# Unread products on TensorE during the first batch entry's attention, and two score banks in place of three

## The chip, the cores and the metric

One NeuronCore of a Trainium2 chip runs the whole program. The metric is the device time in microseconds (us); each kernel has several runs and their median is given. A difference of about 0.2% is what these runs can tell from none. One further execution was recorded by the hardware profiler, and all rows below come from it.

## What is computed

Three parts run one after another on the same 1152 tokens (2 batch entries of 576). The first is an attention of 8 heads, which adds a coarse attention over tokens averaged by fours to a local one with a band mask:

```python
out_d = sm_attn(q_d, k_d, v_d)            # 144 averaged tokens
out_up = np.repeat(out_d, factor, axis=2)
mask = np.abs(pos[:, None] - pos[None, :]) < factor
scores = np.where(mask, scale * np.matmul(q, k.transpose(0, 1, 3, 2)), -1000000000.0)
...
return (out_up + out_local).astype(np.float32)
```

The second is a mixture of 8 experts (512 to 1024 to 512, ReLU, gates balanced by 8 rounds of row and column scaling), the third a dense layer pair (512 to 2048 to 512, softplus).

## The kernel before, in words

**Attention.** A `Unit` is a pair of heads of one batch entry; there are four per entry, eight in all. `load` issues its copies on SyncE (queries and keys into `qk`, values into `vw` and `vd`). `setup(g)`, called for g = 0, 1, 2, transposes three tiles of `qk` on TensorE (line 322) into a PSUM tile `tb`; VectorE sums it by fours (`qkd`, line 327), scales that into `flat` (line 333) and copies half of the queries into `fine` (line 338); ScalarE writes `kT` (line 337) and the other half of `fine` (line 339). `scores(blk)` works on one of four blocks: "c" is the coarse attention (line 355), 0 to 2 are the local one (a mask product in bf16, line 362, and products of `fine` with `kT`, line 368). VectorE takes the maxima (line 375), ScalarE the exponentials (line 379), VectorE sums, reciprocals and the scaling (lines 380 to 382). `turn` transposes the result (lines 393, 402) and ScalarE copies it out (lines 397, 403); `values` multiplies by the values (lines 413, 424) and VectorE adds both attentions (line 439). Blocks go through `scores`, `turn` two blocks later and `values` three blocks later.

**Banks.** `bank("m", ...)` hands out three PSUM banks, `m0`, `m1`, `m2`, in turn. In the first batch entry (`self.b == 0`) the scores of each block take the next of them; in the second entry they use another tag. From the second entry on, `m0` to `m2` serve the experts' first products (line 601, `product`, by the table `places`).

**Overlap.** The loop over `stream` runs the 32 blocks. From block 18 on (`begin`) it also draws from `beside()`, which does the first expert's work on TensorE between the attention of the second entry. In the first entry TensorE has only attention to do. Beside all this, `fetch_first` and `fetch_second` load weights (SyncE) and split them into a high and a low part: ScalarE copies, VectorE (line 133) and GpSimd (lines 111, 139, 154) subtract and add.

**Order.** Tile's scheduler decides the order of each engine's instructions when the program is built, by priorities that follow the order in the source and by a model of when operands are ready. An engine then works through its list strictly in that order. `tc.keep_in_program_order` puts an instruction behind the one that was written before it on the same engine; `tc.high_priority(offset=...)` shifts its priority, and a negative offset makes it less urgent than what stands around it. After the attention, TensorE's order is written out by hand (`manual_schedule`).

Of the kernel before, what the change touches and what calls it, by code (L numbers as in the profile page):

```python
# [9 lines left out]
F32 = mybir.dt.float32  # L10
F32R = mybir.dt.float32r
U32 = mybir.dt.uint32
BF16 = mybir.dt.bfloat16
# [7 lines left out]
def attention_moe_mlp(ctx: ExitStack, tc: tile.TileContext, q, k, v, w_gate, w1, w2, w_in, w_out, out):  # L21
    nc = tc.nc
    B, H, S, D = q.shape
    NT, DM = out.shape
    E, _, FF = w1.shape
    F2 = w_out.shape[0]
    P = 128
# [4 lines left out]
    NQ = S // QT  # L32
    NB = 3
    CT = SD // NB
    KW = QT + 2 * R
    KD = DM // P
    SCALE = 1.0 / float(D) ** 0.5
# [25 lines left out]
    ps = ctx.enter_context(tc.tile_pool(name="ps", bufs=1, space=PSUM))  # L63

    def bank(tag, name):
        if tag == "m":
            tag = f"m{next(turns) % 3}"
        return ps.tile([P, 512], F32, tag=tag, bufs=4 if tag == "at" else 1, name=name)

    turns = count()  # L70
# [182 lines left out]
    at = tc.tile_pool(name="at", bufs=2)  # L253
    ap = at.__enter__()


    identb = ap.tile([P, P], BF16, bufs=1, name="identb")
    nc.vector.tensor_copy(identb, ident)

    mask = ap.tile([P, NB + 2, KW], BF16, bufs=1, name="mask")  # L260
    nc.gpsimd.memset(mask, 0.0)
    for t0, t1, off in ((0, 1, 0), (1, NB + 1, R), (NB + 1, NB + 2, 2 * R)):

        for hh in range(2):
            part = mask[hh * QT : (hh + 1) * QT, t0:t1, :]
            for sign in (1, -1):
                nc.gpsimd.affine_select(
                    out=part, in_=part, compare_op=ALU.is_gt, fill=NEG,
                    base=R + sign * off, pattern=[[0, t1 - t0], [-sign, KW]], channel_multiplier=sign,
                )  # L270
    rest = const.tile([P, KD, LEFT], F32, name="rest")

    fine = [ap.tile([P, NB, 2, QT], F32, bufs=1, name=f"fine{g}") for g in range(NB)]
    flat = [ap.tile([P, NB, 2, CT], F32, bufs=1, name=f"flat{i}") for i in range(2)]
    for x in fine + flat:
        nc.gpsimd.memset(x, 0.0)

    class Unit:
# [9 lines left out]
        def bank(self, name, kind):  # L288
            return bank(("m", "at", "y")[kind] if self.b == 0 else "at", name)

        def load(self, first=False):
# [3 lines left out]
            for cut in cuts:  # L295
                for w, src in enumerate((q, k)):
                    for hh in range(2):
# [3 lines left out]
                        )  # L301
            self.vw = vw = ap.tile([KW, NQ, 2, D], F32, tag="vw", name="vw")
            for t, w0 in ((0, 0), (NQ - 1, S - KW)):
                nc.sync.dma_start(vw[:, t], v[b, h0 : h0 + 2, w0 : w0 + KW, :].rearrange("h p d -> p h d"))
            for hh in range(2):
                src = v[b, h0 + hh, QT - R :, :]
                windows = bass.AP(tensor=src.tensor, offset=src.offset, ap=[[D, KW], [QT * D, NQ - 2], [1, D]])
                nc.sync.dma_start(vw[:, 1 : NQ - 1, hh], windows)
# [40 lines left out]
        def scores(self, blk):  # L349

            sc = self.bank("sc", 0)
            if blk == "c":
                rows, w = 2 * CT, SD
                for i in range(NB):
# [30 lines left out]
        def turn(self, blk):  # L385

            ex = self.state[blk]
            if blk == "c":
                et = ap.tile([HC, 2, NB * 2 * CT], F32, tag="etc", bufs=1, name="etc")
                for c in range(2):  # L390
                    tp = self.bank("tp", 1)
                    for i in range(NB):
                        nc.tensor.transpose(
                            tp[:HC, i * 2 * CT : (i + 1) * 2 * CT], ex[:, i, c * HC : (c + 1) * HC],
                            ident[: 2 * CT, : 2 * CT],
                        )
                    nc.scalar.copy(et[:, c], tp[:HC, : NB * 2 * CT])
            else:
# [65 lines left out]
    def gates():  # L464
        lg = bank("y", "lg")
        for s in range(2):
            lts = pair("lts").rearrange("p a c -> p (a c)")[: 2 * E]
            for j in range(2):
                lt = bank("at", "lt")
                terms = [  # L470
                    (i, w, kk, x[s]) for i, w in (((4, 1), (5, 2)), ((3, 0), (1, 1)))[j]
                    for kk in range(2) for x in (xh, xl)
                ]
                for n, (i, w, kk, x) in enumerate(terms):
                    nc.tensor.matmul(
                        lt[: 2 * E, : HALF[s]], wgs[:, w, kk, :], x[:, i, kk, :],
                        start=(n == 0), stop=(n == len(terms) - 1),
                    )
                nc.scalar.copy(halves(s, lts)[j], lt[: 2 * E, : HALF[s]])
            for t in TILES[s]:  # L480
                o = t * P - T0[s]
                nc.tensor.matmul(lg[:, t * E : (t + 1) * E], lts[:, o : o + P], fold, start=True, stop=True)
        nc.vector.tensor_reduce(m1, lg[:, : NTT * E], axis=AX.X, op=ALU.max)
        nc.vector.tensor_copy(prf, lg[:, : NTT * E])
# [49 lines left out]
    for e, g, s, p in steps:  # L534
        m = e * NP + p
# [205 lines left out]
    for n in range(len(stream) + LAG + 1):  # L741
        if n < len(stream):
            x, blk = stream[n]
            i, j = divmod(n, len(blocks))
            x.scores(blk)
            if j == 1 and 1 <= i <= 6:
                (fetch_first if i % 2 else fetch_second)((i - 1) // 2, (i - 1) // 2)
            if j >= 2 and i + 1 < len(units):
                for g in ((0, 1), (2,))[j - 2]:
                    units[i + 1].setup(g)  # L750
                if j == 3 and i + 2 < len(units):
                    units[i + 2].load()
        for lag, what in ((LAG, "turn"), (LAG + 1, "values")):
            if 0 <= n - lag < len(stream):
                x, blk = stream[n - lag]
                getattr(x, what)(blk)
        while columns < (n - begin) * DENSE:
            columns += next(side, 1 << 30)
# [100 lines left out]
```

## Time and profile before

| | |
|---|---|
| median of 3 runs | 1095.72 us (1094.87 to 1096.78) |
| span of the profiled execution | 1094.7 us, 17873 instructions |
| TensorE matmul busy | 1060.0 us, 97% of the span |
| VectorE / ScalarE / GpSimd busy | 727.0 / 555.2 / 537.6 us |
| first product of an expert (line 601) starts | 66.70 us |

The profiled span lies 1.0 us below the median, and within 0.2 us of the fastest run. The page gives busy time by engine, and in 40 slices also the clock that TensorE was granted (tenths of full speed). In the rows, PE is TensorE's matmul queue, PEld its weight loads, DVE VectorE, ACT ScalarE, POOL GpSimd and SP SyncE; in a group of instructions the mean duration of one stands behind the busy time. An interval written in square brackets is idle time ahead of an instruction, with what ended it.

### The profile page before, as it was taken

The page shows a single profiled execution, that of the slowest core. Times are in us where ns is not written, and L with a number is a line of the kernel's source. Part 1 is how long each engine was busy: PE and PEld are TensorE (multiplying, and loading weights), DVE is VectorE, ACT ScalarE, POOL GpSimd, SP SyncE. Part 2 cuts the span into 40 slices and gives each one's busy share as a digit, 9 for nine tenths or more (in the row PEclk, how much of TensorE's full clock was granted, in tenths as well). Part 3 has the DMA queues.
Part 4 walks back from the last instruction along what each step waited for, and adds up shares of the span by engine and source line. Part 5 has one row for each costly group of instructions (what it writes and reads, how often), then busy time and mean ns, then how long its engine had stood idle before and what let it go on. Part 6 is the DMA issues. An engine that isn't in the chain of part 4 may idle for free.

```text
span 1094.7 us, 17873 instructions
## 1 busy us (share of the span) xinstructions
PE 1060.0 (97%) x6385; PEld 938.0 (86%) x6385; DVE 727.0 (66%) x1532; ACT 555.2 (51%) x1443; POOL 537.6 (49%) x569
## 2 busy tenths in 40 slices
PE   6899999999999999999999999999999998999998
PEld 5678888998987889888888988898898897889987
DVE  6889665565666676667657665766663578766765
ACT  4667645343444444434444443444443567676763
POOL 6735235464467676756766455354664212222321
PEclk9579999999999999999999999999999999999999
DMA  8454101111235334434443332223333273244112
GB/s 175 118 115 109 49 27 55 62 58 40 84 100 145 115 110 143 132 105 127 122 134 102 117 112 93 100 93 110 102 116 116 106 278 139 113 175 182 68 39 87
DMA packets 133497, 119.70 MB, mean 109 GB/s; under 512 B 35744, under 2 KB 111776, under 8 KB 133408
## 3 DMA queue, kind: packets, MB, share of 16 engines
q1 hardware_dynamic: 133408, 118.56, 35.0%
q8 instruction: 50, 0.82, 0.3%
q14 instruction: 39, 0.32, 0.1%
HBM read 93.11 MB, written 25.43 MB: 108 GB/s over the span
## 4 chain that ended last, share of the span: by engine, by line
PE 40%; POOL 5%; DMA 5%; DVE 3%; issue 2%; ACT 2%; SPq 0%; POOLq 0%; ACTq 0%; DVEq 0%
PE yps L660 21%; PE m L601 19%; DMA raw<-in_moe_w_out 2%; POOL sums L111 2%; POOL w2l L154 1%; POOL cva L188 1%; POOL cva L197 1%; DMA raw<-in_moe_w 1%; DMA raw<-in_moe_w_in 1%; DVE cva L178 1%; POOL w1l L139 1%; DVE cva L189 0%; DVE cva L179 0%; DVE cva L182 0%; DMA s_out<-cva 0%
## 5 line engine op out<-in xcount | busy, mean ns | idle before, releaser
L601 PE MATMUL m<-xh,w1h 128*128 128x320 f32 (+1 forms) x1120 | 336.6, 301 | 13.1 <-ACT t L610 6.3
L601 PE MATMUL m<-xh,w1l 128*128 128x320 f32 (+1 forms) x1120 | 332.5, 297 | 0.0
L601 PE MATMUL m<-xl,w1h 128*128 128x320 f32 (+1 forms) x1120 | 332.4, 297 | 0.0
L601 PEld LDWEIGHTS m<-xh,w1h 128*128 128x128 f32 x1120 | 212.2, 189 | 38.7 <-ACT t L610 10.8
L601 PEld LDWEIGHTS m<-xl,w1h 128*128 128x128 f32 x1120 | 212.4, 190 | 11.8
L601 PEld LDWEIGHTS m<-xh,w1l 128*128 128x128 f32 x1120 | 212.2, 190 | 0.2 <-issue 0.2
L660 PE MATMUL yps<-w2h,hh 128*128 128x512 f32 x502 | 198.5, 395 | 0.0
L660 PE MATMUL yps<-w2l,hh 128*128 128x512 f32 x502 | 198.4, 395 | 0.0
L660 PE MATMUL yps<-w2h,hl 128*128 128x512 f32 x502 | 195.5, 389 | 0.0
L660 PE MATMUL yps<-w2h,h 128*128 128x512 f32 x436 | 153.3, 393 | 0.0
L615 DVE TENSOR_TENSOR c<-m,t 128x256 f32<-128x256 f32 (+1 forms) x160 | 72.3, 452 | 100.9 <-PE m L601 99.5
L139 POOL TENSOR_TENSOR w1l<-sums,w1h 128x512 fp32r<-128x512 f32 x72 | 95.8, 1345 | 78.2 <-ACT w1h L138 54.4
L571 POOL TENSOR_TENSOR ab<-ab,up 128x320 f32<-128x320 f32 (+1 forms) x64 | 53.9, 843 | 157.2 <-ACT ln L567 109.8
L154 POOL TENSOR_TENSOR w2l<-raw,w2h 128x512 fp32r<-128x512 f32 x72 | 94.9, 1339 | 71.4 <-ACT w2h L153 71.3
L558 ACT ACTIVATE hh<-c 128x256 fp32r<-128x256 f32 (+1 forms) x138 | 60.0, 443 | 125.0 <-DVE c L615 123.3
L559 DVE SCALAR_TENSOR_TENSOR hl<-c,hh 128x256 fp32r<-128x256 f32 (+1 forms) x138 | 91.4, 668 | 35.0 <-ACT hh L558 33.2
L660 PEld LDWEIGHTS yps<-w2h,hl 128*128 128x128 f32 x502 | 94.4, 188 | 21.3
L677 DVE SCALAR_TENSOR_TENSOR acc<-yps,pr,acc 128x512 f32<-128x512 f32 x117 | 86.9, 743 | 29.5 <-PE yps L660 29.4
L660 PEld LDWEIGHTS yps<-w2h,hh 128*128 128x128 f32 x502 | 94.7, 189 | 12.6 <-DVE acc L673 0.2
L660 PEld LDWEIGHTS yps<-w2l,hh 128*128 128x128 f32 x502 | 94.7, 189 | 11.1 <-issue 0.4
L660 PEld LDWEIGHTS yps<-w2h,h 128*128 128x128 f32 x436 | 82.6, 189 | 14.8
L188 POOL TENSOR_TENSOR cva<-cva,raw 128x512 uint32<-128x512 uint32 x32 | 42.7, 1336 | 95.2 <-DVE raw L185 76.6
(134 smaller groups left out, 1700.7 us busy)
## 6 DMA issues: line engine op xcount, KB each, us to landing
raw<-in_moe_w SPq DMA_DIRECT2D x72, 256.0 KB
raw<-in_moe_w SPq DMA_DIRECT2D x36, 512.0 KB
w1h<-s_in SPq DMA_DIRECT2D x10, 896.0 KB
w1l<-s_in SPq DMA_DIRECT2D x10, 896.0 KB
raw<-in_moe_w_in SPq DMA_DIRECT2D x32, 256.0 KB
raw<-in_moe_w_out SPq DMA_DIRECT2D x16, 512.0 KB
w2l<-s_out SPq DMA_DIRECT2D x10, 512.0 KB
w2h<-s_out SPq DMA_DIRECT2D x10, 512.0 KB
```

The lines of the kernel that those rows point to most:

```text
L111: nc.gpsimd.tensor_tensor(sums[i], a, b, op=op)
L139: nc.gpsimd.tensor_tensor(lo[:, part], sums, hi[:, part].bitcast(F32), op=ALU.subtract)
L154: nc.gpsimd.tensor_tensor(lo[:, i], raw[:, i], hi[:, i].bitcast(F32), op=ALU.subtract)
L178: nc.vector.tensor_scalar(a, high, 0x07FFFFFF, 3, op0=ALU.bitwise_and, op1=ALU.logical_shift_left)
L188: nc.gpsimd.tensor_tensor(a, a, low, op=ALU.add)
L558: nc.scalar.activation(hh, c, AF.Relu)
L559: nc.vector.scalar_tensor_tensor(out=hl, in0=c, scalar=0.0, in1=hh.bitcast(F32), op0=ALU.max, op1=ALU.subtract)
L571: nc.gpsimd.tensor_tensor(ab, ab, up, op=ALU.subtract)
L601: nc.tensor.matmul(b[:, :h], x[:, i, kk, :], y[s][:, i, kk, :], start=(not more and n == 0), stop=(n == 5), skip_group_check=more,)
L615: nc.vector.tensor_tensor(c, b[:, :h], t, op=ALU.add)
L660: nc.tensor.matmul(y, a[:, f, tok], b[:, f, :], start=(start and m == 0), stop=(stop and m == 5))
L677: nc.vector.scalar_tensor_tensor(out=acc[t], in0=y, scalar=pr[:, t, e : e + 1], in1=acc[t], op0=ALU.mult, op1=ALU.add,)
```

## The change

A constant bf16 tile `warm` of 128x512 ones is written by VectorE. `keep_warm(n)` issues n matrix products of 128x128 by 128x512 of that tile into one PSUM tile `idle`, which nothing reads. Fourteen stand ahead of everything on TensorE; three stand behind the scores of each of the 16 blocks of the first batch entry, each in program order behind the instruction written before it, and with a priority lowered by 60. The tile `idle` takes the bank `m2`, so that `bank("m", ...)` alternates between `m0` and `m1`.

```diff
+    START, BETWEEN, LOW = 14, 3, -60
...
         if tag == "m":
-            tag = f"m{next(turns) % 3}"
+            tag = f"m{next(turns) % 2}"
...
+    warm = ap.tile([P, 512], BF16, bufs=1, name="warm")
+    nc.vector.memset(warm, 1.0)
+    idle = ps.tile([P, 512], F32, tag="m2", name="idle")
+
+    def keep_warm(n):
+
+        for _ in range(n):
+            tc.keep_in_program_order(nc.tensor.matmul(idle, warm[:, :P], warm, start=True, stop=True))
+
+    keep_warm(START)
...
             x.scores(blk)
+            if x.b == 0:
+                with tc.high_priority(offset=LOW):
+                    keep_warm(BETWEEN)
```

## Rows read from the trace of the kernel before

**Rows 1.** The page: busy by engine; granted clock in 40 slices of 27.4 us.
```profile
PE 1060.0 (97%) x6385; PEld 938.0 (86%) x6385; DVE 727.0 (66%) x1532; ACT 555.2 (51%) x1443; POOL 537.6 (49%) x569
...
PEclk9579999999999999999999999999999999999999
```

**Rows 2.** Stretches from unit to unit: length, busy (count) by engine, clock, DMA share, GB/s.
```profile
7.52:14.50 6.98, 5.88 (x27) 5.20 (x25) 5.56 (x17) 2.99 (x12) 2.23 (x4) 1.00 0.85 160
14.50:28.20 13.70, 11.73 (x72) 9.41 (x73) 12.83 (x31) 9.79 (x40) 10.44 (x12) 1.00 0.89 209
28.20:46.60 18.40, 13.93 (x97) 10.98 (x97) 15.39 (x38) 12.93 (x55) 12.89 (x15) 0.61 0.64 151
46.60:63.40 16.80, 15.89 (x98) 12.71 (x98) 15.78 (x42) 9.53 (x36) 12.21 (x17) 0.50 0.59 112
```

**Rows 3.** One form of PE's products in 6.5 to 26, 26.5 to 33.5, 33.6 to 66.3.
```profile
L368 PE MATMUL sc<-kT,fine 128*128 128x72 f32 x25 | 5.4, 384 | 0.8 <-ACT fine L339 0.8
...
L368 PE MATMUL sc<-kT,fine 128*128 128x72 f32 x8 | 1.2, 278 | 0.0
...
L368 PE MATMUL sc<-kT,fine 128*128 128x72 f32 x33 | 8.2, 404 | 0.0
```

**Rows 4.** Stretches around the changes of the granted clock.
```profile
30.00:32.64 2.64, 0.92 (x16) 0.66 (x14) 2.56 (x9) 2.64 (x13) 2.64 (x5) 0.93 0.10 26
...
57.00:66.40 9.40, 9.40 (x61) 8.47 (x60) 9.08 (x24) 5.28 (x26) 6.68 (x9) 0.50 0.79 140
...
76.00:78.40 2.40, 0.37 (x12) 0.24 (x9) 0.73 (x4) 2.40 (x17) 0.00 (x0) 1.00 0.69 133
...
80.43:86.90 6.47, 6.22 (x34) 5.53 (x33) 6.37 (x25) 3.71 (x15) 0.77 (x1) 0.50 0.40 92
```

**Rows 5.** What DVE waited for, 6 to 67 us: total, times, longest.
```profile
DVE qkd L327 <- PE tb L322: 6.2, 3, 5.6
DVE small L375 <- PE sc L355: 2.3, 2, 1.5
DVE xf L439 <- PE pv L424: 1.3, 1, 1.3
```

**Rows 6.** 512-column products in the chain; 256-column ones in PE's timeline.
```profile
781.99 1.39 PE yps L660 x6
...
84.19 0.41 PE L601 MATMUL m<-xh,w1l 128*128 128x256 f32 x1
84.41 0.41 PE L601 MATMUL m<-xh,w1h 128*128 128x256 f32 x1
```

**Rows 7.** Timeline of the start: first VectorE work, transposes of three units.
```profile
0.83 0.17 DVE L83 MEMSET ones<- 128x128 f32 x1 [0.83 <-PEq L844]
...
6.61 2.15 PE L322 MATMUL tb<-ident,qk 128*128 128x128 f32 x9 [6.61 <-POOL mask L267]
14.45 1.54 PE L322 MATMUL tb<-ident,qk 128*128 128x128 f32 x6 [0.27 <-DMA qk<-in_k]
28.19 0.82 PE L322 MATMUL tb<-ident,qk 128*128 128x128 f32 x6
```

**Rows 8.** Timeline around the fourth unit's scores and the first expert product.
```profile
62.71 1.17 DVE L375 TENSOR_REDUCE small<-sc 96x3 f32<-96x432 f32 x3
...
64.07 0.37 ACT L379 ACTIVATE ex<-sc,small 96x144 f32<-96x144 f32 x1
...
65.67 0.34 ACT L379 ACTIVATE ex<-sc,small 128x72 f32<-128x72 f32 x1
...
66.70 0.36 PE L601 MATMUL m<-xh,w1h 128*128 128x256 f32 x1
```

**Rows 9.** One form on DVE twice, and what POOL did beside the first.
```profile
33.54 3.70 DVE L382 TENSOR_TENSOR ex<-ex,small 128x216 f32<-128x216 f32 x1
...
39.53 0.37 DVE L382 TENSOR_TENSOR ex<-ex,small 128x216 f32<-128x216 f32 x1
...
33.83 2.48 POOL L154 TENSOR_TENSOR w2l<-raw,w2h 128x512 fp32r<-128x512 f32 x2
```

## The prediction

> **What bounds the kernel now.** The page comes first: TensorE is busy for 97% of the span, so over most of the kernel its work alone sets the end, and the granted clock is full in all but the first four slices [rows 1]. Whatever the first stage gives up or takes is therefore carried to the end: the experts' products start earlier or later by that much, and nothing behind them has slack for TensorE to lose it in, or little. So the stage to read is the one from the start to the first expert product at 66.70 us [rows 8].
>
> Second, the stretches from one unit's transposes to the next [rows 2]. In the last of them TensorE is busy for 15.89 of 16.80 us and VectorE for 15.78: two engines are full at once. In the third both have gaps. The clock column says 0.61 and 0.50 there, so TensorE's share is work at the lower of its two levels (1.2 GHz). For the first 26 us the column says 1.00, but the durations say otherwise: the same product, 128x72, takes 384 ns up to 26 us, 278 ns from 26.5 to 33.5 us and 404 ns from 33.6 to 66.3 us [rows 3]. I read the first as half level before the first recorded change. So the first entry ran at full level for some 7 us of 60.
>
> Third, what the clock did around its changes [rows 4]. It fell just after a stretch with 0.92 us of work in 2.64, and again after one with 0.37 in 2.40. It stayed at half through 57 to 66.40 us with TensorE busy all the time on attention's products and transposes. It was at half again from 80.43 to 86.90 us, with the experts' 256-column products mixed in (two of them in [rows 6]), and the page's slices from there on are at 9 tenths or more [rows 1].
>
> Fourth, VectorE's waits [rows 5]. Leaving out the first 5.6 us, in which there was no data, the waits at the head of its list all ended with a product or transpose of TensorE: 0.6 us for line 322 (6.2 less 5.6), 2.3 for line 355 and 1.3 for line 424.
>
> **The ceiling.** If TensorE were never late, the stage could not be shorter than VectorE's work, whose durations do not hang on TensorE's clock. VectorE's idle time by stretch is 6.98 - 5.56 = 1.42, 13.70 - 12.83 = 0.87, 18.40 - 15.39 = 3.01 and 16.80 - 15.78 = 1.02 us, together 6.3 us [rows 2]. That, and some tenths at the start, is what a faster clock can give, although it halves far more of TensorE's own time.
>
> **The products behind the scores.** 16 blocks by 3 make 48. No product of this kind is in the trace; the nearest by width is 128x512, six of which took 1.39 us at full level, 0.232 us each [rows 6]. At half level two 256-column products start 0.22 us apart, which makes 0.44 us for 512 [rows 6]. So the 48 cost 11.1 us of TensorE at full level and 21 us at half. At full level there is room: the last three stretches hold 41.6 us of TensorE work in 48.9 us [rows 2], and the transposes show what the level is worth (six take 1.54 us at 14.45 and 0.82 at 28.19 [rows 7]); about half of the 41.6 us falls away. What can still cost is a group of three that stands ahead of a product whose operands have just come: at most 0.70 us a block, 11.1 us for all 16, at least nothing. With the lowered priority they are queued where TensorE is expected to be idle, so I take 0.3 us, and keep the upper end for a rival.
>
> **What the clock gives.** I take it stretch by stretch. First: the next unit's transposes at 14.45 us waited for the copy of its keys [rows 7], so most of the 1.42 us is not TensorE's to give; the nine first transposes, 2.15 us, would take about 1.2, which frees VectorE some 0.3 us earlier: 0.3. Second: TensorE is behind part of 0.87: 0.4. Third: the two long waits, 1.5 us for line 355 and 1.3 us for line 424 [rows 5], come at the end of unbroken half-level work and would halve or vanish: 2.2 of 3.01. Fourth: 0.7 of 1.02. Together 3.6 us, between nothing and 6.6.
>
> **The fourteen at the start.** They need the constant tile, which VectorE can write once it starts at 0.83 us; a 128x128 fill took 0.17 us there [rows 7], so the wider one should take 0.2 to 0.7 us. From about 1.3 us on, the fourteen take 3.2 us at full level and 6.2 at half, and end between 4.5 and 7.5 us, while the first transposes start at 6.61 [rows 7]. They overhang by 0 to 0.9 us, and they are what could lift the clock for unit 0; I take nothing for them on either side. SyncE's copies are untouched: its first queue entries depend on none of this.
>
> **Two score banks for three.** The fourth unit shows what a third bank is for: VectorE takes three blocks' maxima in a row at 62.71 us, while ScalarE's third exponential of the first of these blocks starts at 64.07 and the third block's exponentials at 65.67 [rows 8]. With two banks the third block's scores can only start when the first's exponentials are read, about 64.6 us. Its six products of line 368 at 278 ns [rows 3] overlap, so they take between 0.3 (one) and 1.7 us (six in a row); I take 1.0, and 0.4 for the maxima (1.17 / 3), which brings its exponentials to about 66.0: some 0.4 us late for that block. Four units make 0 to 1.6 us where only ScalarE is late, and up to 4 us if what is queued behind those scores on TensorE (transposes and value products of earlier blocks) is held too. One more thing moves: with three banks the experts' first product finds `m1` free since block 13; counted by two, `m1` belongs to block 15, whose exponentials come about 2 us after its scores. The first product may start up to 2 us later, but TensorE is nearly idle at 76.0 to 78.4 us [rows 4], which takes that up. For all of it I take 0.6 us.
>
> **The sum.** -3.6 + 0.3 + 0.6 = -2.7 us. The profiled span lies 1.0 us below the median, so the change is applied to the median: 1095.7 - 2.7 = 1093.0 us.
>
> **Rival one: the clock rises, and the stage is no shorter.** VectorE's and GpSimd's instructions hold each other up: line 382 took 3.70 us at 33.54 and 0.37 at 39.53, and the first lay beside a run of GpSimd subtractions from 33.83 us on [rows 9]. Such a stretch moves with the work but does not go away, and an earlier product only meets it sooner; the idle time returns as a longer instruction. Then 0 to 1 us remains, less the banks: 1095.4 us. Thirty in a hundred. The Trainium skill (SBUF — State Buffer, "Summary: rules for kernel authors") says that of a VectorE instruction with two SBUF inputs and a GpSimd one that reads SBUF, the one issued second is fully blocked until the first ends; by that rule the time would come out as this rival does. The trace agrees in the 3.70 us above; it doesn't show that all stretched instructions would stay so.
>
> **Rival two: the products don't lift the clock, and it is slower.** The place is TensorE from 14.5 to 63.4 us. At half level the twelve products of a unit take 12 x 0.44 = 5.3 us; TensorE's work per stretch becomes 17.0, 19.2 and 21.2 us, against lengths of 13.70, 18.40 and 16.80 [rows 2]: 3.3 + 0.8 + 4.4 = 8.5 us more, 1104.2 us. It decides from the point at which half level holds in most of the stage; where it holds in half of it, the loss and the gain are about equal. For it speaks that 9.40 us of unbroken work left the clock at half [rows 4]; against it that the clock came back behind the stretch from 80.43 us, in which 256-column products like those of [rows 6] were mixed into the same attention. Fifteen in a hundred, with three of these for a milder form in which the clock is full but groups of three stand in the way.
>
> **Rival three: more than forecast.** All of VectorE's idle time goes, and its stretched instructions fall better: 6.6 us, 1089.1 us. Seven in a hundred.
>
> **How the numbers follow.** The forecast has 48 in a hundred; its own range is 1090 to 1094.5. A measurement of this kernel tells about 0.2%, 2.2 us, from no change. Faster by more than that: 42 of the forecast's 48, and the 7 of rival three: 0.49. Within it: 5 of the forecast's, 27 of rival one, 2 of rival two: 0.34. Slower: 1, 3 and 13: 0.17. The range takes in rival three's time and the milder form of rival two, and leaves out most of its full form: 1089 to 1099 us.
>
> **What would show it.** Right: a granted clock at or near 1.00 from 30 to 66 us, line 368 near 280 ns there; VectorE's waits for lines 355 and 424 under half of what they are; the first expert product at about 64 us. The clock for the first 26 us has to be read from durations. The banks would show as mask products (line 362) waiting for ScalarE. Wrong: the clock at half behind the products, TensorE full and the first expert product after 68 us; or a full clock with VectorE as busy as its stretch is long, and the first expert product where it was.

## The result, and the profile after

The changed kernel takes 1107.91 us (median of 4 runs, 1105.47 to 1113.34) against 1095.32 us for the kernel before on the same chip: a ratio of 1.0121, with a 95% interval of 1.01 to 1.0143. It is slower by about 13 us, where 1093.0 us was forecast, and lies above the range's upper end of 1099. The profiled execution has a span of 1106.4 us; its time was 1108.14, and in each run on record the time lies some 1.8 us above the span of the same execution. So the profiled execution of the kernel before took about 1096.5 us by this measure, and lay a little above its median.

In the changed file all lines of the attention class and behind it stand 12 lower: the transposes of line 322 are line 334, the sums of line 327 are line 339, the scores of lines 355 and 368 are lines 367 and 380, the mask products of line 362 are line 374, the gate weights' sum of line 459 is line 471. The unread products are line 265.

The page of the changed kernel; busy by engine and granted clock, to be read against [rows 1].

```profile
span 1106.4 us, 17994 instructions
...
PE 1066.8 (96%) x6447; PEld 934.7 (84%) x6447; DVE 733.9 (66%) x1533; ACT 555.8 (50%) x1443; POOL 537.7 (49%) x569
...
PEclk8789999999999999999999999999999999999999
```

TensorE is busy for 6.8 us more, VectorE for 6.9, and the span is 11.7 us longer: there is more waiting too. The second row is where to look first. These are the stretches of [rows 2] in the changed kernel; columns as there.

```profile
14.50:28.20 13.70, 10.48 (x58) 6.65 (x57) 10.85 (x18) 7.34 (x33) 9.28 (x12) 0.75 0.58 132
28.20:46.60 18.40, 14.40 (x111) 10.82 (x113) 14.98 (x45) 13.16 (x48) 10.24 (x12) 0.78 0.47 121
46.60:63.40 16.80, 12.96 (x101) 8.59 (x99) 14.81 (x34) 9.93 (x41) 10.49 (x13) 0.80 0.68 144
```

From 14.5 to 28.2 us VectorE gets through 18 instructions where it got through 31 [rows 2], and TensorE through 58 where it got through 72, unread ones included. The stage falls behind here. The next view says how far: TensorE's timeline, the first transposes of each unit, the unread products ahead of them and the first expert product. Columns: start, duration (overlapping instructions together), engine, line, operation, count, and in brackets the idle time before.

```profile
1.60 4.84 PE L265 MATMUL idle<-warm 128*128 128x512 bf16 x14 [1.60 <-DVE warm L259]
6.41 1.17 PE L334 MATMUL tb<-ident,qk 128*128 128x128 f32 x9
...
15.29 2.77 PE L265 MATMUL idle<-warm 128*128 128x512 bf16 x6
...
18.95 0.81 PE L265 MATMUL idle<-warm 128*128 128x512 bf16 x3
19.60 0.82 PE L334 MATMUL tb<-ident,qk 128*128 128x128 f32 x6
...
38.26 0.82 PE L334 MATMUL tb<-ident,qk 128*128 128x128 f32 x6
...
54.99 0.87 PE L334 MATMUL tb<-ident,qk 128*128 128x128 f32 x6
...
73.66 0.82 PE L334 MATMUL tb<-ident,qk 128*128 128x128 f32 x6
...
76.59 0.47 PE L613 MATMUL m<-xh,w1h 128*128 128x256 f32 x1
```

The transposes stood at 6.61, 14.45 and 28.19 us [rows 7], and the third and fourth following unit began at 46.62 and 63.40 (the bounds of [rows 2]). So the loss is -0.2, +5.2, +10.1, +8.4 and +10.3 us: it arises between the first and the third unit, and the fourteen products at the start have no part in it by their length, since the first transposes are even 0.2 us earlier. It then travels to the end. The first of the later transposes that the expert part makes for its gates is a mark that stands at a fixed place of the work; one line of each kernel, before and after, with durations in ns and the start in us:

```profile
L491 PE MATMUL m<-ident,m x1: 271/271/271, 180.1 to 180.1; 128*1 128x128 f32 x1
```

```profile
L503 PE MATMUL m<-ident,m x1: 271/271/271, 188.8 to 188.8; 128*1 128x128 f32 x1
```

That is 8.7 us of the span's 11.7. The rest comes later, some tenths at a time over hundreds of us, and wasn't taken apart. I call this place the **first mark** below. Behind it lie 917.6 us here and 914.6 before. In the four executions further down that hold the lists of before it is 915.3 to 918.8, so these last 3 us can't be told from the difference between executions.

TensorE's waits in the changed kernel, 6 to 77 us: what it waited for, total, times, longest.

```profile
PE sc L367 <- DVE qkd L339: 9.9, 3, 4.5
PE pv L425 <- DVE xf L451: 2.1, 1, 2.1
PE tb L334 <- ACT etc L409: 1.6, 1, 1.6
PE sc L374 <- ACT ex L391: 1.2, 1, 1.2
```

9.9 us in three waits, all of coarse scores for the sums of a unit's set-up on VectorE. The same view of the kernel before (6 to 67 us), and the start of the second unit's sums on its VectorE timeline:

```profile
PE sc L355 <- DVE qkd L327: 0.9, 2, 0.8
...
15.39 0.56 DVE L327 TENSOR_REDUCE qkd<-tb 128x96 f32<-128x384 f32 x1 [0.34 <-PE tb L322]
```

There the wait was 0.9 us in all. So TensorE, which now runs faster, stands waiting for VectorE, and the changed kernel's VectorE timeline shows why: sums of the first two units, and what stands around them.

```profile
6.97 0.56 DVE L339 TENSOR_REDUCE qkd<-tb 128x96 f32<-128x384 f32 x1 [5.02 <-PE tb L334]
...
10.14 0.62 DVE L471 TENSOR_TENSOR wg<-wg 128x16 f32<-128x16 f32 x1 [2.61 <-DMA wg<-in_moe_w_gate]
10.68 0.54 DVE L339 TENSOR_REDUCE qkd<-tb 128x96 f32<-128x384 f32 x1
...
21.18 1.01 DVE L339 TENSOR_REDUCE qkd<-tb 128x96 f32<-128x384 f32 x2
...
23.04 5.21 DVE L134 TENSOR_TENSOR w1l<-raw,w1h 128x512 fp32r<-128x512 f32 x1
28.17 0.40 DVE L345 TENSOR_SCALAR flat<-qkd 64x48 f32<-64x48 f32 x2
```

Three things stand out. The gate weights' sum (line 471) waits 2.61 us for its copy, ahead of the second sum of the first unit, whose transposes are done. The second unit's sums start at 21.18 us instead of 15.39. And a subtraction of an expert's weights, which no product reads before 76.59 us, takes 5.21 us in front of the second unit's remaining work; beside it GpSimd works without a pause:

```profile
23.30 2.49 POOL L155 TENSOR_TENSOR w2l<-raw,w2h 128x512 fp32r<-128x512 f32 x2
25.75 0.72 POOL L112 TENSOR_TENSOR sums<-raw,sums 128x256 f32<-128x256 f32 x1
26.43 1.26 POOL L140 TENSOR_TENSOR w1l<-sums,w1h 128x512 fp32r<-128x512 f32 x1
```

None of these three instructions is new. **What is new is their place in the list of their engine.** The planner that orders the kernel's instructions was given 62 more on TensorE, one more on VectorE and one bank less, and it made another list for every engine. VectorE's list as planned, from the first unit's set-up on (`...` where instructions are left out; `qkd`, `flat`, `fine` are a unit's set-up, `small`, `ex` its exponentials):

```
before                                  after
qkd                                     qkd
flat x2                                 wg         (gate weights, line 471)
qkd                                     qkd
fine                                    flat x2
qkd                                     qkd
...                                     ...
small 96x3, small 128x3 x2, small       small 96x3, small 128x3, small
qkd        (second unit)                small, ex, small 128x3, small, small, ex
...                                     qkd x2     (second unit)
fine x2    (second unit)                ...
w1l 128x256                             w1l 128x512
ex x2, qkd                              flat x2    (second unit)
w1l 128x512                             ...
```

On TensorE likewise: the second unit's transposes stood ahead of the first unit's last block of scores; now they stand behind all four blocks and nine unread products.

Of the 1532 instructions that both VectorE lists have, only the last 260 stand in the same order as before, counted from the end; the list differs far behind the edit, in the experts' part too.

### The profile page after: what moved, and what is told of

Same layout as the page of the kernel before. It is cut to its first block, busy times and chain, and to the rows that moved or that the text cites. A ratio compares the mean times of both kernels' runs of the same rounds, so it can differ in the third digit from the quotient of the medians.

```text
span 1106.4 us, 17994 instructions
## 1 busy us (share of the span) xinstructions
PE 1066.8 (96%) x6447; PEld 934.7 (84%) x6447; DVE 733.9 (66%) x1533; ACT 555.8 (50%) x1443; POOL 537.7 (49%) x569
## 4 chain that ended last, share of the span: by engine, by line
PE 35%; POOL 6%; DMA 6%; DVE 4%; issue 3%; ACT 2%; SPq 0%; POOLq 0%; DVEq 0%; ACTq 0%
PE yps L672 19%; PE m L613 16%; POOL sums L112 2%; DMA raw<-in_moe_w_out 2%; DMA raw<-in_moe_w 1%; POOL w2l L155 1%; POOL cva L189 1%; POOL cva L198 1%; DMA s_out<-cva 1%; DVE cva L179 1%; POOL w1l L140 1%; DMA s_in<-cva 1%; DVE cva L180 1%; DMA raw<-in_moe_w_in 1%; DVE cva L190 1%
## 5 line engine op out<-in xcount | busy, mean ns | idle before, releaser
L613 PEld LDWEIGHTS m<-xh,w1h 128*128 128x128 f32 x1120 | 212.7, 190 | 41.6 <-ACT t L622 12.6
L672 PEld LDWEIGHTS yps<-w2h,h 128*128 128x128 f32 x436 | 82.4, 189 | 14.8
```

The source lines that it names most:

```text
L613: nc.tensor.matmul(b[:, :h], x[:, i, kk, :], y[s][:, i, kk, :], start=(not more and n == 0), stop=(n == 5), skip_group_check=more,)
L672: nc.tensor.matmul(y, a[:, f, tok], b[:, f, :], start=(start and m == 0), stop=(stop and m == 5))
```

## The experiments

The suspects at first were the bank that is taken away and the instructions that came to stand badly (the gate weights' sum above all); the order as a whole became the theory in the course of them. "Mark" is the first mark's time in that run's profile, 180.1 us in the kernel before. All ratios are to the kernel before.

**One part at a time.** Two banks alone:

```diff
-            tag = f"m{next(turns) % 3}"
+            tag = f"m{next(turns) % 2}"
```

> Only the banks of the first entry's scores go from three to two; no product is added. Theory A (the third bank was what held the scores ahead of the exponentials): most of the 12 us appears here, 1101 to 1107 us, with score products waiting for ScalarE. Theory B (the added work shifts the planned order of VectorE, ahead of which things now stand that arrive late): VectorE's first fourteen instructions are in the order of before, so little happens, 1094 to 1098 us. Theory C (TensorE's time in the products): 1095 us.

Measured 1104.66 us, 1.0073 [1.0049, 1.0097], mark 184.0. No product was added, and some 60% of the loss is there. Theory A named this number, but not what the trace shows: no wait of TensorE for ScalarE's exponentials is in it from 6 to 77 us. What grew is the wait for the sums of a set-up, 0.9 us in the kernel before:

```profile
PE sc L355 <- DVE qkd L327: 5.8, 2, 5.3
```

The fourteen at the start alone, with three banks:

```diff
-    START, BETWEEN, LOW = 14, 3, -60
+    START, BETWEEN, LOW = 14, 0, -60
-            tag = f"m{next(turns) % 2}"
+            tag = f"m{next(turns) % 3}"
```

> The fourteen products ahead of the first transposes alone, three banks, none behind the scores. Theory B: the gate weights' sum (wg) stands in VectorE's list ahead of the second group of transposes, as in the changed kernel, and waits there some 2.6 us for its copy; 1098 us or more. Theory A: 1095 us. Theory C: 1095 to 1096 us, since the fourteen end at about 6.4 us, where the first transposes start anyway.

1101.44 us, 1.0046 [1.0028, 1.0063], mark 180.8. Costed at nothing, they come to about 5 us, though they are over when the transposes begin. In the profiled execution the span is 6.3 us longer, and only 0.7 us of that is there at the first mark; 920.2 us lie behind it, where TensorE, VectorE, ScalarE and GpSimd work through the lists of before (they agree from 140 us on). What made that part longer is not shown.

The products behind the scores alone, with two banks (`START, BETWEEN = 0, 3`):

> The three products behind each block's scores alone, with two banks, none at the start; wg stands where it stood before. Theory A: as slow as the two banks alone, 1101 to 1107 us. Theory B: some 3 us less than the changed kernel, near 1104 us, or 1096 to 1100 if the start is most of it. Theory C: nearly all of the loss, 1105 to 1108 us.

1106.31 us, 1.0089 [1.0067, 1.011], mark 182.6. By the ratios the fourteen cost about 5.0 us and these products, with two banks, 9.8 us; together 14.8, which the whole change's 13.3 can't be told from. Here too the larger part, 9.4 of the 11.9 us by which the span is longer, comes behind the first mark (924.0 us).

All 62 products, the third bank given back; the products write a bank of the transposes' tag:

```diff
-            tag = f"m{next(turns) % 2}"
+            tag = f"m{next(turns) % 3}"
-    idle = ps.tile([P, 512], F32, tag="m2", name="idle")
+    idle = ps.tile([P, 512], F32, tag="at", bufs=4, name="idle")
```

> All 62 products, but the unread tile lies in one of the four banks that take transposes, so that the scores keep three banks. Theory A: 1095 to 1098 us. Theory B: wg still stands in front; 1098 us or more. Theory C: 1105 to 1108 us as in the changed kernel.

1101.9 us, 1.0051 [1.0036, 1.0065], mark 182.7: it gives back 6 us by the medians. And the same without the fourteen (`START = 0`):

> The 48 products behind the scores with three score banks, none at the start. Theory A (banks): against the same products with two banks, 1106.3 us, most of the 10 us goes, 1096 to 1099 us. Theory D (any new plan costs some 5 us): 1100 to 1103 us. Theory C (TensorE's time in the products): 1105 us.

1106.28 us, 1.0077 [1.0054, 1.01], mark 186.0. With the products behind the scores alone, two banks (1.0089) and three (1.0077) can't be told apart; the fourteen, which cost 5 us alone, don't cost anything beside the others: without them the three-bank kernel is 4 us slower by the medians (the intervals overlap). So neither the bank nor the fourteen has a price of its own; what each costs hangs on what else is there. An order made anew for each kernel could do that, and a fixed wait for a bank could not.

**The gate weights' sum moved back.** In three kernels the sum, its copy and its subtraction are written behind the first unit's set-up and held there:

```diff
-    nc.vector.tensor_tensor(wg[:, 0], wg[:, 1], wg[:, 2], op=ALU.add)
...
         units[0].setup(g)
+    tc.keep_in_program_order(nc.vector.tensor_tensor(wg[:, 0], wg[:, 1], wg[:, 2], op=ALU.add))
...
     units[1].load()
```

In the kernel with all products and three banks:

> All 62 products with three score banks (as in the run with three banks), and the gate weights' sum held behind all three set-ups of the first unit in VectorE's list. Theory B (what was planned in front waits): its wait of 2.1 us is gone and 2 to 3 us come back, 1098.5 to 1100 us. Theory D (the rest of the new plan costs the same whichever instruction is in front): 1101 to 1103 us. If the clock is worth what was forecast once nothing stands in the way: 1093 to 1095 us.

1109.77 us, 1.011 [1.0079, 1.0141], mark 189.3: 7.9 us worse by the medians than without the move. In the kernel with the fourteen alone:

> The fourteen products at the start alone, three banks, the gate weights' sum held behind the first unit's set-ups. Theory B: 1098 to 1099 us against 1101.4 with the sum in front. Theory D: 1100 to 1102 us. If the start only gives a warmer clock: 1095 us.

1097.31 us, 1.001 [0.9995, 1.0025], mark 175.3: 4.1 us better, and no loss is left. And in the kernel before:

> A control: the kernel before, with the gate weights' sum one place later in VectorE's list and nothing else. Theories A to C: 1095 to 1097 us, as before. Theory D (the order before is a lucky one, and any other costs): 1099 us or more.

1094.59 us, 0.9987 [0.9972, 1.0002]: no difference. One move made one kernel worse, one better, and one neither. The sum's own wait, which the move takes away, was 2.10 us in the first kernel without the move, 2.42 us in the second, and nothing in the kernel before, where the sum already stood behind the third of the unit's sums and its copy had landed. So the third result was to be expected: there the lists of TensorE and GpSimd stayed as they were, and VectorE and ScalarE each have one instruction in another place. The wait can't explain the first two together; in both, the lists of TensorE, VectorE, ScalarE and GpSimd came out new around the move. And a new list isn't dear by being new: that of the second kernel agrees with the list of before in only the first 4 and the last 1244 of VectorE's 1532 instructions, and costs nothing that can be told.

**The order held.** The next kernels take the planner out. Every engine's list, as it was planned for one kernel, is written out as numbers, and each instruction gets an edge to the one ahead of it in the list that orders the two and adds no wait:

```diff
+        for x, y in zip(made, made[1:]):
+            tc.add_manual_dep(y, x.name, info, reason="plan")
...
+    replay(tc, extra, fronts)
```

First the list of the kernel before, with nothing else, to see what the holding costs:

> The kernel before with its own order held by the same means as in the runs with a held order; nothing else. All theories: 1094 to 1097 us. Its profile is a second look at the same program, and tells by how much the attention and the hand-ordered stage differ from execution to execution.

1096.58 us, 1.0005 [0.999, 1.0019], mark 179.9: nothing that can be told. The trace shows every engine in the order of before.

Then the list of before with all 62 products in it, and three banks: fourteen in front, and three ahead of each of the first entry's blocks of scores, written to the scores' own bank:

```diff
+    fronts.append((extra[:1] + keep_warm(ps.tile([P, 512], F32, tag="m2", name="idle"), START), None))
...
+            made = keep_warm(sc, BETWEEN if self.b == 0 else 0)
...
+                fronts.append((made, mm.ins))
```

> The order of every engine is held as in the kernel before, three score banks, and the 62 products are put into it: fourteen in front, three ahead of each block's scores in the first entry, written into the bank that the scores then overwrite. Nothing else changes. Theory E (the loss is the new order, and the clock is worth what was forecast): 1091 to 1095 us. Theory C (the products cost TensorE time on the path): 1100 us or more. If the clock is full and gives nothing: 1095 to 1098 us.

1095.76 us, 1.0009 [0.9992, 1.0026], mark 174.8. **In the old order the products, with whatever their clock gives, come to nothing that can be told.** That is price and gain together; this run doesn't part them. Their place is that of the change as far as the old order has it (ahead of a block's scores, not behind the block before). What they do to the clock is plain in the durations of the 128x72 product of [rows 3]; here it is for 6.5 to 26 and 26.5 to 66 us, in this kernel and then in the held list without the products:

```profile
L552 PE MATMUL sc<-kT,fine 128*128 128x72 f32 x25 | 3.4, 272 | 0.3 <-ACT fine L519 0.3
...
L552 PE MATMUL sc<-kT,fine 128*128 128x72 f32 x45 | 7.6, 302 | 0.0
```

```profile
L538 PE MATMUL sc<-kT,fine 128*128 128x72 f32 x18 | 4.4, 416 | 0.8 <-ACT fine L509 0.8
...
L538 PE MATMUL sc<-kT,fine 128*128 128x72 f32 x48 | 11.8, 410 | 0.0
```

272 and 302 ns against 416 and 410: full level, or near it, against half. A quarter to a third off every such product, and the time is the same.

With the three products ahead of each block's value products instead, in that tile's bank:

> The same held order of before and the same 62 products, but the three of a block stand ahead of its value products, in their bank, where TensorE waits for ScalarE's copies. Theory E: 1091 to 1095 us. Theory C: 1098 us or more, less than ahead of the scores if they fall into waits. If the clock gives nothing: 1095 to 1097 us.

1098.69 us, 1.0027 [1.0013, 1.0041], mark 177.7: 3 us more than before; that the place of the products makes the difference isn't shown, since the two intervals overlap.

The profile of the kernel with the products at the scores fell 3.2 us below that of before (span 1091.5), close to the 2.7 us that had been forecast. It was taken again:

> The order of before with the 62 products ahead of the scores, a second time. If the clock's gain in the attention is real, the first transpose of the gates (180.1 us in the trace of before) lies near 175 us again, as in the first of these runs (174.8), and the end between 1093 and 1097 us; if that look was a lucky one, 178 us or more.

1095.57 us, 0.9997 [0.9979, 1.0014], mark 182.1. The very same program was at the first mark 7.3 us later in this execution. Its VectorE timeline, and GpSimd beside it, then TensorE's longest wait (6 to 77 us):

```profile
29.97 2.09 DVE L564 TENSOR_SCALAR small<-small 96x3 f32<-96x3 f32 x1
32.77 3.51 DVE L564 TENSOR_SCALAR small<-small 128x3 f32<-128x3 f32 x1
...
33.08 2.49 POOL L323 TENSOR_TENSOR w2l<-raw,w2h 128x512 fp32r<-128x512 f32 x2
...
PE tp L577 <- DVE ex L566: 6.4, 2, 5.7
```

An instruction over 3 numbers a row, whose median is 0.17 us, takes 2.09 and 3.51 us while GpSimd works without a pause; the transposes of the coarse attention's result wait 5.7 us for the scaling behind it, a wait of at most 1.2 us in the first execution. One profile of this stage is therefore no measure of it; the runs of this kernel spread from 1092.95 to 1102.51 us.

The last cell of the square: the changed kernel's list on every engine, two banks, the products left out of it (they are the only work left out):

> The order of every engine is held as in the changed kernel, with its two score banks, and the 62 products and their constant tile are left out. Theory E: as slow as the changed kernel or slower, since the clock is missing too, 1106 to 1112 us. Theory C: back to 1095 to 1099 us. A mixture: 1100 to 1105 us.

1110.93 us, 1.0132 [1.0107, 1.0157], mark 191.3. **The order with the two banks, without any of the products, has the whole loss.** TensorE's waits, 6 to 77 us, and the instruction on VectorE behind which they stand:

```profile
PE sc L524 <- DVE qkd L496: 10.0, 3, 4.0
...
23.43 5.21 DVE L302 TENSOR_TENSOR w1l<-raw,w1h 128x512 fp32r<-128x512 f32 x1
```

They are the same 10 us in three waits and the same 5.21 us as in the changed kernel. With three banks in that list (`% 3`):

> The order of the changed kernel on every engine, without the products, as in the run that took 1110.9 us, but the scores get their third bank back. Theory A' (the two banks' waits on the chip are a large part, whatever the order): 1102 to 1107 us. Theory E (the order alone): 1109 to 1112 us, with a few waits of TensorE for ScalarE gone and nothing else.

1109.19 us, 1.0119 [1.0102, 1.0136], mark 187.9; 8.4 of the 10.0 us in those waits remain. On the chip, then, the third bank is worth some 1.4 us by the two ratios (0.0013 of 1096), and that isn't told apart from none. **The order alone has the rest**, 1.0119 against the changed kernel's 1.0121.

**Which instructions of the order.** In the changed kernel, list held and products in, the 5.21 us subtraction alone is moved behind the second unit's set-up in VectorE's list; in a second kernel the gate weights' sum also moves, behind the third of the first unit's sums:

```diff
-        "0 2 1 3 6 4 10 7-8 14 9 5 11-13 15-17 55 18 22 19-21 26 23-25 30 34 27 31-32 38 35-36 28 33 37 29 42 "
+        "0 2 1 3 6 10 7-8 14 9 4-5 11-13 15-17 55 18 22 19-21 26 23-25 30 34 27 31-32 38 35-36 28 33 37 29 42 "
```

(the second one's line of VectorE's list against the first's: the gate weights' sum is number 4.)

> The changed kernel in its own order, products and all, with one VectorE instruction moved: the second subtraction of the first expert's low part (w1l, 128x512), which took 5.21 us beside GpSimd there and held up the second unit's set-up, goes behind that set-up. Theory F (that one instruction in front is worth its stall): 3 to 4.5 us come back, 1103.5 to 1105 us. Theory G (the loss is spread over the order and a stall moved is a stall kept): 1106.5 to 1109 us.

> As the run before it, and the gate weights' sum also goes from ahead of the second group's sum to behind the third's. Theory F: another 2 to 2.6 us, 1101 to 1103 us. Theory G: 1105.5 to 1109 us, as the wait at the start is covered by the copy of the next unit's keys.

1105.89 us, 1.0085 [1.0056, 1.0115], mark 183.1; and 1104.85 us, 1.0081 [1.006, 1.0102], mark 183.3. Two to three us by the medians against the changed kernel's 1107.91, about 4 by the ratios, with intervals that overlap its own; some 5.5 us at the first mark in one execution each. Both lie between what theories F and G had said. (The changed kernel's list, held with nothing moved, was not run.) In the second kernel VectorE's timeline has another instruction in the subtraction's place:

```profile
22.12 4.42 DVE L563 TENSOR_TENSOR ex<-ex,small 128x216 f32<-128x216 f32 x1
```

Its length there is 4.42 us; the same form took 0.37 and 3.70 us in [rows 9]. There the stall went to what VectorE had at hand beside GpSimd's run. In the first kernel it did not: no VectorE instruction between 20 and 33 us took more than 1.05 us, and one took 2.44 at 33.83. So the two instructions account for a part; **the other 9 us or so of the order's cost I have not brought down to single instructions**, and they stay open. In the second kernel's profile 3.2 of the 6.2 us that are left in the span are there at the first mark, and 3.0 come behind it.

## Why the prediction was wrong

The four corners, times in us:

| | without the products | with the products |
|---|---|---|
| order of before | 1096.6 (three banks) | 1095.8, 1095.6 (three banks) |
| order of after | 1110.9 (two), 1109.2 (three) | 1107.9 (two) |

The ratios, each to the kernel before on the same chip, are 1.0005, then 1.0009 and 0.9997, in the first row, and 1.0132 and 1.0119, then 1.0121, in the second.

**The step that failed** is in the change part by part: "With the lowered priority they are queued where TensorE is expected to be idle, so I take 0.3 us", "SyncE's copies are untouched", and a sum that has terms for TensorE's time and for banks alone. It took every other engine's list for fixed and put their change at nothing, without a reason. The kernel's lists are computed from all of its instructions, SyncE's too, which agrees with that of before in its first 13 and last 328 of 414 entries; and the new lists cost 12.6 us by the left column with three banks (1109.2 less 1096.6) and 14.3 with two, some five times the sum of -2.7, with the other sign. No rival held that; the slower one was about the half level of the clock, and that did not come: its condition failed, and its 1104.2 us is nearer to the result only by chance.

**Price and gain of the products.** In the held old order the two terms that belong to them, -3.6 for the clock and 0.3 for the groups, came to 0 (1.0009 and 0.9997, each with about 1.8 us on either side), where -3.3 was forecast. So a second step was mis-sized too, and which of the two isn't separated: the groups may have cost what the clock gave. That they can have a price is seen where they stand ahead of the value products: 1.0027, clear of the kernel before by its interval. In the new order the kernel with products is about 1 us shorter by the ratios (1.0121 against 1.0132), and the two intervals overlap. Of the costed details: the fourteen were to end between 4.5 and 7.5 us and ended at 6.44 (1.60 + 4.84), with the first transposes at 6.41; the banks were to show as mask products waiting for ScalarE, and one did for 1.2 us, beside the 0.6 us taken and about 1.4 measured. Unread groups stand in a row in the timeline (six from 15.29 us, three at 18.95), the last of them right ahead of the second unit's transposes.

**The clock rose, by less than forecast, and the time did not follow.** The granted clock was 0.75 to 0.80 in the stretches where it had been 1.00 (on record), 0.61 and 0.50; at or near 1.00 was forecast. From 30 to 66 us the 128x72 product took 332 ns, not near 280. VectorE's waits for coarse scores and value products came to 1.7 and 0.8 us, against 2.3 and 1.3 before [rows 5], and were to be under half.

```profile
L380 PE MATMUL sc<-kT,fine 128*128 128x72 f32 x42 | 7.7, 332 | 0.0
...
DVE small L387 <- PE sc L367: 1.7, 2, 0.9
DVE xf L451 <- PE pv L436: 0.8, 1, 0.8
```

In the held old order the product came down from 410 to about 300 ns in most of the stage. What the traces hold there speaks for **rival one**, without proving it: VectorE's busy time from 6 us to the first expert product, in the held list without the products and in the two executions with them (columns: stretch, length, busy and count, clock, DMA share, GB/s).

```profile
6.00:67.56 61.56, 50.60 (x132) 1.00 0.69 148
...
6.00:64.07 58.07, 52.96 (x132) 0.88 0.71 157
...
6.00:70.36 64.36, 55.38 (x136) 0.87 0.65 142
```

In the first execution the first expert product came at 64.07 us, as forecast: VectorE's idle time fell from 11.0 to 5.1 us, while the same 132 instructions of the same list took 2.4 us more. In the second its idle time was 9.0 us, but its instructions were longer still, 2.09 and 3.51 us on one whose median is 0.17, and the product came at 70.36. The ceiling of 6.3 us of VectorE's idle time was read from one execution, and the next execution moves more than that by itself (7.3 us at the first mark). The rule that the prediction weighed (the Trainium skill, SBUF — State Buffer, "Summary: rules for kernel authors": of a VectorE instruction with two SBUF inputs and a GpSimd one that reads SBUF, the one issued second is blocked until the first ends) agrees in kind with 5.21 and 4.42 us beside GpSimd's runs, but not in length: each lasted across several GpSimd instructions of 0.5 to 1.4 us. The 3.51 us are those of an instruction with a single tensor input, which is not the case that the prediction named.

**"What would show it"** named the first expert product at 64 us if right and after 68 if wrong. It came at 76.59. The sign was good; of the two ways to be wrong listed with it, neither was the one, since the clock was up and VectorE less busy than before in the second stretch (10.85 of 13.70 us against 12.83, [rows 2]).

What stays open: which places in the new lists cost the remaining 9 us; whether the products save anything in the new order; whether their price or the clock's gain was off in the old one; and why the kernel with the fourteen alone, and the one with the products behind the scores alone, lose most of their time behind the first mark. A list of the two-bank kernel without products, held and run with three banks, was not tried; so for that part alone (1104.66 us) only its waits speak on order against bank.

## What to carry to other kernels

Where a planner orders the instructions, an edit may be more than what it adds: compare the planned lists of every engine before costing it, and to test the idea itself, hold the old lists and put the new instructions into them. A list that differs is a warning and no price: one new list here cost 13 us and another nothing. Work that kept the clock up was worth nothing that could be told in this stage, where VectorE was nearly as full as TensorE; look first whether another engine's stalls would take the place of TensorE's time. And read a stage of this kind from several executions: one profile here stood 3.2 us below the kernel before and the next one 6.0 above it.

## What the runs showed of the hardware that was not expected

- **The clock's record can say full where the durations say half.** In the kernel held in the old order without products the page shows no slice below 9 tenths, while the 128x72 products took 416 and 410 ns all through the first entry, against 270 to 303 in the two executions with products. Here is that page's row; the level has to be read from durations where no change is on record.

```profile
PEclk9999999999999999999999999999999999999999
```

- **A VectorE instruction can last across several of GpSimd's.** The same 128x512 subtraction took 5.21 us in the changed kernel at 23.04 us, across four GpSimd instructions in a row, and 0.69 us later in that VectorE timeline:

```profile
42.08 0.69 DVE L134 TENSOR_TENSOR w1l<-raw,w1h 128x512 fp32r<-128x512 f32 x1
```

- **The same program differs by 7.3 us at its first mark** (174.8 and 182.1 us) between two executions, in which VectorE's long instructions are other ones.
